# VectorE exponentials as a sum of three shifted 16-bit patterns, in a fused two-branch attention kernel

## The chip, the cores and the metric

The kernel runs on one core of one Trainium2 chip. Its time is device microseconds of one launch; the median of 7 runs of the kernel before is 780.64 us (779.15 to 784.05). Beside it stands one execution recorded by the hardware profiler, and all durations below come from that one.

## The reference, cut to what matters

Two attention branches read the same `x` (2048 rows, 512 columns, 32 heads of 16) and are mixed by a gate. Branch B is softmax attention, branch A is linear attention with a softmax feature map.

```python
def _B_ref(x, wqkv, wo):
    ...
    scores = jnp.einsum("bhqd,bhkd->bhqk", q, k) * (Dh ** -0.5)
    p = _softmax(scores, axis=-1)
    o = jnp.einsum("bhqk,bhkd->bhqd", p, v)
    return (lambda x, *d: x.transpose(*d))(o, 0, 2, 1, 3).reshape(B, S, D) @ wo

g = _sigmoid((x * gate_w).sum(-1, keepdims=True))
a = _A_ref(x, A_wqkv, A_w_phi, A_wo)
b = _B_ref(x, B_wqkv, B_wo)
return g * a + (1 - g) * b
```

What costs most is branch B: 32 heads times 2048 x 2048 scores, each of which needs an exponential. The sum that the softmax divides by is a column of ones beside the values, so numerator and denominator come from the same matmuls, and a common factor on all exponentials cancels.

## The kernel before, in words

**Tiles and blocks.** A tile is 128 keys by 512 queries of one head, so 64 tiles belong to one block of four heads and one query chunk, and there are 32 blocks (`NB`). TensorE makes the scores of a tile with one matmul that uses 32 of the array's rows (`qk_mm`, L782), the exponentials are taken, and TensorE multiplies them with the values, using 32 of its columns per head, into the one accumulator bank `psO` (`pv_mm`, L895). Four matmuls on different 32-row or 32-column strips can run side by side. At the end of a block VectorE copies `psO` out (L979) and the next block starts.

**Two makers of exponentials.** Most tiles go to ScalarE in slots of three and two tiles by turns: `add_qk` fills three PSUM banks (or two), `add_exp` (L874) turns them into bf16 in one of ten parts of `Ebuf`, `add_pv` consumes them some slots later. There are 637 such slots. The other tiles, `DN[b]` of each block and 456 in all, go to VectorE in groups of four (106 groups) or two (16). For one group `add_group` lists: one scores matmul per tile (called dq below) into a spare PSUM bank, D1 (L840) that adds a constant and rounds to int16, so that the 16 bits read as bf16 are a rough power of two; D2 (L855), which takes the low bits and joins a fixed exponent to them; D3 (L857), which keeps the high bits; and D4, which multiplies the first by the second, on VectorE (L860) or, for the first one or two groups of a block (`PN`), on GpSimd in quarters (L863). `add_pvd` then adds two matmuls per tile into `psO`, called terms below: one of the product (`t`) and one of the high bits (`s`).

**Buffers.** Each group holds three buffers of 128 x 2048 bf16: `t`, `s` and the scratch `m`. They come from `rings`, with one set for blocks before `G_EARLY` (13) and one for those after it. `t` and `s` turn through four and four buffers, later four and three. `m` has two fixed ones, one for groups whose product is on VectorE and one for those on GpSimd; it is free again once the product is done. `make_groups` lists a group only when the terms of the earlier holders of its buffers have been listed.

**Order.** All work of all engines is a list of operations with a duration, a priority and dependencies. `layout` runs through them once at build time and fixes the order on every engine; `emit` writes that order out with semaphore waits. [...] When `layout` finds nothing for TensorE and its weighted use over the last 3.41 us is below a bound, it puts in four matmuls of a zero weight (`zero_mm`, L885): they add nothing to the accumulator. VectorE's D2, D3, D4 and GpSimd's tensor operations are marked `lock`, and `layout` doesn't let those of one engine overlap those of the other.

**The rest.** Projections, branch A (its feature map takes 64 more ScalarE exponentials, L1117, sums and products on GpSimd, L1122 and L1130) and the output tiles (`out_tile`, `out_part`, `out_last`; matmuls L590, scaling L1041 and L1065) lie between the slots. The last block ends with a transpose on VectorE, a reciprocal, a product and a second transpose, and then the last matmul of each of the output tiles 12 to 15.

Of the kernel before, what the change touches and what calls it, by code (L numbers as in the profile page):

```python
# [11 lines left out]
ALU = mybir.AluOpType  # L12
# [11 lines left out]
VAW = H * VW + 16  # L24
LOG2E = 1.4426950408889634
QSCALE = 0.25 * LOG2E * 2.0 ** 7
EXPB = 127.0 * 2.0 ** 7 - 75.0
ESCALE = math.log(2.0) / 2.0 ** 7

DN = (0, 10, 14, 16, 14, 16, 14, 16, 14, 16, 14, 16, 14, 16, 14, 16, 14, 16, 14, 16, 14, 16, 14, 16, 14, 16, 14, 16, 14, 16, 14, 12)  # L30
# [72 lines left out]
class Plan:  # L103
# [8 lines left out]
    def add(self, eng, dur, prio, fn, reads=(), writes=(), after=(), name="", sem=None, lat=0.0):  # L112
        op = Op(eng, max(dur - 0.105, 0.05) * DVE_SCALE if eng == "dve" else dur, prio, fn, name)
        if eng == "dve":
            lat += 0.08
        elif eng == "act" and sem is None:
            lat += 0.04
        elif eng == "pe":
            op.dur = max(dur - 0.04, 0.05)
            lat += 0.1  # L120
        op.seq = len(self.ops)
        op.sem, op.lat = sem, lat
        deps = {}
        for k in reads:
            w = self.writer.get(k)
            for x in w or ():
                deps[id(x)] = x
        for k in writes:
            for x in self.writer.get(k) or ():
                deps[id(x)] = x  # L130
            for x in self.readers.get(k, ()):
                deps[id(x)] = x
        for x in after:
            deps[id(x)] = x
        op.deps = list(deps.values())
        for k in reads:
            self.readers.setdefault(k, []).append(op)
        for k in writes:
            self.writer[k] = [op]
            self.readers[k] = []  # L140
        self.ops.append(op)
        return op
# [258 lines left out]
def _build(ctx, nc, A_x, A_wqkv, A_w_phi, A_wo, B_wqkv, B_wo, gate_w, out):  # L401
# [71 lines left out]
    P = Plan()  # L473
# [20 lines left out]
    for rr in range(8):  # L494
# [4 lines left out]
                  name="woa", lat=5.0),  # L499
              dma("sp", 2.2, lambda e: e.dma_start(WoB[:], B_wo.rearrange("(t p) c -> p t c", p=128)), ["WoB"],  # L500
                  name="wob", lat=5.0)]
# [3 lines left out]
    def warm_fn(e):  # L505
        ins = None
        for _ in range(6):
# [5 lines left out]
    pool = lambda dur, prio, fn, reads=(), writes=(), name="": P.add("pool", dur, prio, fn, reads=reads,  # L513
                                                                    writes=writes, name=name)
# [3 lines left out]
         writes=["ident"], name="ident")  # L518
# [9 lines left out]
          writes=["pmask0"], name="pm0")  # L528
    P.add("dve", 0.1, -9, lambda e: e.tensor_scalar(pmask[:, 1:2], pmask[:, 0:1], -QSCALE, QSCALE, op0=ALU.mult,
                                                    op1=ALU.add), reads=["pmask0"], writes=["pmask1"], name="pm1")  # L530
    P.add("dve", 0.1, -9, lambda e: e.tensor_single_scalar(pmask[:, 0:1], pmask[:, 0:1], QSCALE, ALU.mult),
          reads=["pmask1"], writes=["pmask", "pmask0"], name="pm2")
# [6 lines left out]
    for t in range(KT):  # L539
# [12 lines left out]
          writes=["mtmp1"], name="mk0")  # L552
    P.add("dve", 0.12, 30, lambda e: e.tensor_single_scalar(mask64[:], m1, 16, ALU.is_lt), reads=["mtmp1"],
          writes=["mask64"], name="mk1")
    pool(0.3, -2, lambda e: e.tensor_copy(mask4[:], mask64[:].rearrange("p (j c) -> p j c", c=16)[:, :, 0]),
         reads=["mask64"], writes=["mask4"])
# [176 lines left out]
    for j, act in enumerate(slots):  # L733
        for t in act:
            last_act[t[0]] = t
            first_slot.setdefault(t[0], j)
    I16 = mybir.dt.int16
# [6 lines left out]
            "a0": (vfree[:, 0, :], va_free), "a1": (vfree[:, 1, :], va_free),  # L744
            "a2": (vfree[:, 2, :], va_free), "a3": (vfree[:, 3, :], va_free)}
    bufs["pq"], bufs["pt"] = (flat(phiQ[:]), ()), (phiQT[:].rearrange("p g q -> p (g q)"), ())
    rings = ((("x0", "x1", "pq", "o3"), ("y0", "y1", "pt", "o2"), ("woA", "woB")),
             (("x0", "x1", "n0", "a0"), ("y0", "y1", "a1"), ("a2", "a3")))
    for k in range(1):
        bufs[f"n{k}"] = (flat(WAT[:, 4 * k:4 * k + 4, :]), wp_ops)  # L750
# [1 line left out]
    for n, g in enumerate(groups):  # L752
        g["n"], g["ph"] = n, (g["ts"][-1]["t"][0] >= G_EARLY)
        rt, rs, rm = rings[g["ph"]]
        g["m"] = rm[g["pool"]]
        k = count[g["ph"]]
        count[g["ph"]] += 1
        g["t"], g["s"] = rt[k % len(rt)], rs[k % len(rs)]
        for q, d in enumerate(g["ts"]):
            d["g"], d["q"] = g, q  # L760
    opened, phase_ops = set(), [[], []]

    def opening(name):
        if name in opened:
            return []
        opened.add(name)
        return list(bufs[name][1])

    def quarter(ap, q):
        if len(ap.shape) == 3:  # L770
            return ap[:, q // 2, 512 * (q % 2):512 * (q % 2) + 512]
        return ap[:, 512 * q:512 * q + 512]

    def shaped(ap, like):
        return ap.rearrange("p (a c) -> p a c", c=1024) if len(like.shape) == 3 and len(ap.shape) == 2 else ap
# [37 lines left out]
    holder = {}  # L813

    def make_groups(n):
        for g in groups[made[0]:n]:
            if any(k in holder and holder[k]["left"] for k in (g["t"], g["s"])):
                break
            holder[g["t"]] = holder[g["s"]] = g
            add_group(g)  # L820
            made[0] += 1

    def d_prio(d):
        b = d["t"][0]
        return first_slot[b] + d["k"] * 20.0 / DN[b] - D_AHEAD

    def add_group(g):
        t, s, m = (bufs[g[k]][0] for k in "tsm")
        ft, ops, tb = opening(g["t"]), [], t
        before = list(dq_ops)  # L830
        dq_ops.clear()
        for q, d in enumerate(g["ts"]):
            b, i, kt = d["t"]
            f, mm = fill(DQ_PRIO + DQ_K * d_prio(d), [lambda e, ap, t=d["t"]: qk_mm(e, t, ap)],
                         [kkey(b // 8, kt), ("q", b // 2 % 4, b % 2)], name=f"dq{b}.{kt}.{i}", dur=0.25,
                         after=[exp_ops[D_FIRST]] + ft + P.writer.get((g["t"], q), []) +
                         P.readers.get((g["t"], q), []) + before, cols=NQ)
            dq_ops.append(mm)
            mm.kind, mm.heads = "dq", [i]
            ops.append(drain(f, mm, "dve", 0.70, d_prio(d), lambda e, ap, q=q: e.tensor_scalar(  # L840
                quarter(tb, q).bitcast(I16), ap, EXPB, 0.0, op0=ALU.add, op1=ALU.max),
                writes=[(g["t"], q)], after=ft, name=f"D1.{b}.{kt}.{i}"))

        def add(dur, fn, reads, writes, name, after=()):
            ops.append(P.add("dve", dur, d_prio(g["ts"][0]) - 5.0, fn, reads=reads, writes=writes, after=after,
                             name=f"{name}.{b}.{kt}"))
            ops[-1].lock = True
        size = len(g["ts"])
        part = lambda ap: ap[:, 0:512 * size] if len(ap.shape) == 2 else ap[:, 0:size // 2, :]
        t4, m4 = t, m  # L850
        t, s, m = part(t), part(s), part(m)
        tk = [(g["t"], k) for k in range(size)]
        mi, si16, ti16 = m.bitcast(I16), s.bitcast(I16), t.bitcast(I16)
        full = size == 4
        add(0.72 if full else 0.45, lambda e: e.tensor_scalar(shaped(mi, mi), shaped(ti16, mi), 0x007F, 0x3F00, op0=ALU.bitwise_and,  # L855
                                            op1=ALU.bitwise_or), tk, [g["m"]], "D2", opening(g["m"]))
        add(0.72 if full else 0.45, lambda e: e.tensor_single_scalar(shaped(si16, si16), shaped(ti16, si16), 0x7F80, ALU.bitwise_and),  # L857
            tk, [g["s"]], "D3", opening(g["s"]))
        if not g["pool"]:
            add(1.24 if full else 0.72, lambda e: e.tensor_tensor(shaped(t, m), shaped(t, m), m, ALU.mult), [g["m"]], tk, "D4")  # L860
        else:
            for q in range(4):
                ops.append(P.add("pool", 1.1, d_prio(g["ts"][0]) - 5.0, lambda e, q=q: e.tensor_tensor(  # L863
                    quarter(t4, q), quarter(t4, q), quarter(m4, q), ALU.mult), reads=[g["m"]], writes=[tk[q]],
                    name=f"D4{q}.{b}.{kt}"))
                ops[-1].lock = True
        if g is groups[-1]:
            last_d1.extend(ops[:size])
        phase_ops[g["ph"]].extend(ops)
# [28 lines left out]
    def add_pvd(d, started):  # L898
        g, q, (b, i, kt) = d["g"], d["q"], d["t"]
        ops = []  # L900
        for which in "st":
            ap = quarter(bufs[g[which]][0], q)
            op = P.add("pe", 0.25, T_PRIO, lambda e, ap=ap: pv_mm(e, (b, i, kt), ap, False, False),
                       reads=[(g["t"], q) if which == "t" else g["s"], ("v", b // 8, kt // 4), "v1", "v2"],
                       after=[started], name=f"pvd{which}{i}.{b}.{kt}")
            op.full = 0.215
            op.kind, op.heads = "term", [i]
            ops.append(op)
        g["left"] -= 1
        phase_ops[g["ph"]].extend(ops)  # L910
        return ops
# [301 lines left out]
    for i in range(4):  # L1213
        mms = [lambda e, ap, i=i, t=t: e.transpose(ap.bitcast(BF16)[:, 128 * t:128 * (t + 1)],
                                                   xs[:, i, 128 * t:128 * (t + 1)], ident[:]) for t in range(KT)]
        f, mm = fill(-1.0, mms, [("xs", i), "ident"], FIRST, name=f"X{i}", chunk=4, dur=0.08, cols=128)
        x_mms.append(mm)
        dst = xT[:, :, 128 * i:128 * (i + 1)]
# [96 lines left out]
    for op in P.ops:  # L1315
        if op.name.endswith(".0") and op.name[:-2] in gates:
            op.deps = op.deps + [exp_ops[gates[op.name[:-2]]]]
        for head, at, pace in (("P1.", KG_AT, KG_PACE), ("VA", KG_AT, KG_PACE), ("P0.", QG_AT, QG_PACE)):
            part = op.name[len(head):].split(".")
# [38 lines left out]
```

## Time and profile before

| what | value |
|---|---|
| median of 7 runs | 780.64 us (779.15 to 784.05) |
| the profiled execution's own time | 781.83 us |
| span from its first to its last instruction | 780.0 us |
| granted TensorE clock, mean | 0.989 |
| VectorE: D2 (L855), D3 (L857), D4 (L860), busy | 92.0, 88.8, 87.7 us (122, 122 and 75 instructions) |
| GpSimd: D4 in quarters (L863), busy | 215.9 us (188 instructions) |
| TensorE: zero matmuls (L885) | 1764 in the program, 154.2 us busy |
| TensorE: matmuls into `psO` (L895) | 2504 in the program, 239.0 us busy |

The busy time of an engine is the union of its instructions' intervals. Successive instructions of one engine overlap somewhat in this record, so a count times a mean is more than a busy time. The span is 1.8 us shorter than the time of the same execution; the difference lies around the first and the last instruction.

### The profile page before, as it was taken

Reading aid. Unit: us, or ns where it says so; the run is one execution under the profiler, and the core shown is the slowest. Engines: PE = TensorE matmul, PEld = TensorE weight load, DVE = VectorE, ACT = ScalarE, POOL = GpSimd, SP = SyncE. Lnnn points to the kernel's source line nnn. Section 1 sums busy time; section 2 is a strip of 40 time slices with the busy share of each in tenths; the row PEclk is TensorE's granted clock in tenths of the full one; section 3 lists DMA queues with packets and bytes.
Section 4 is the critical chain, followed back from the end, with each engine's and each line's share of the span. In section 5 each row is a group of like instructions: output and inputs, shape, how many; then the busy total and the mean of one; then the engine's idle time right before and its main releaser. Section 6 shows DMA issues by size and latency. Waiting matters only on the chain.

```text
span 780.0 us, 17608 instructions
## 1 busy us (share of the span) xinstructions
PE 741.3 (95%) x7285; PEld 231.3 (30%) x7342; DVE 674.8 (87%) x1098; ACT 758.7 (97%) x708; POOL 352.2 (45%) x329
## 2 busy tenths in 40 slices
PE   8999999999999999999999999999999999999999
PEld 4332223322332222333222232223223223222223
DVE  3678898889989898889999899999999899788793
ACT  6999999999999999999999999999999999989995
POOL 6223634536354564442744636564363544104332
PEclk9999999989999999999999999999999999989999
DMA  7600000000000100201001312331321221020001
GB/s 129 143 9 17 21 13 20 9 18 12 10 17 10 23 8 9 71 9 23 23 23 46 74 56 56 60 68 53 73 66 58 57 63 43 26 52 16 23 21 48
DMA packets 67935, 30.74 MB, mean 39 GB/s; under 512 B 53208, under 2 KB 62808, under 8 KB 67856
## 3 DMA queue, kind: packets, MB, share of 16 engines
q1 hardware_dynamic: 66368, 28.95, 15.7%
q8 instruction: 57, 0.93, 0.5%
q10 hardware_dynamic: 1104, 0.66, 0.3%
q0 software_dynamic: 384, 0.02, 0.1%
q14 instruction: 22, 0.18, 0.1%
HBM read 7.87 MB, written 8.88 MB: 21 GB/s over the span
## 4 chain that ended last, share of the span: by engine, by line
ACT 73%; PE 21%; DVE 4%; issue 1%; DMA 1%; SPq 0%; DVEq 0%
ACT E_t L874 70%; PE psS L782 6%; PE psO L895 5%; ACT EA_t L1117 4%; PE psO L885 3%; PE psS L590 2%; PE psM L590 2%; DVE Tx_t L840 1%; PE psM L782 1%; DMA phiK_t<-in_A_x_dram 1%; DVE vA_t L840 0%; DVE WAT_t L840 0%; DVE oA_t L1205 0%; DVE vA_t L855 0%; DVE Ty_t L857 0%
## 5 line engine op out<-in xcount | busy, mean ns | idle before, releaser
L874 ACT ACTIVATE E_t<-psS 128x1536 bf16<-128x1536 f32 x637 | 729.9, 1339 | 7.8 <-PE psS L782 7.0
L782 PE MATMUL psS<-qz_t,kTB_t 32*128 32x512 bf16 x1816 | 287.3, 387 | 25.6 <-ACT E_t L874 19.2
L863 POOL TENSOR_TENSOR Tx_t<-Tx_t,vA_t 128x512 bf16<-128x512 bf16 x116 | 132.9, 1167 | 124.6 <-DVE Ty_t L857 46.4
L885 PE MATMUL psO<-xT_t,zero_t 128*32 128x512 bf16 x1720 | 151.5, 386 | 0.0
L782 PEld LDWEIGHTS psS<-qz_t,kTB_t 32*128 32x128 bf16 x1816 | 71.4, 91 | 251.7 <-ACT E_t L874 196.1
L895 PE MATMUL psO<-E_t,vaug_t 128*32 128x512 bf16 (+1 forms) x1592 | 140.5, 389 | 0.9 <-issue 0.5
L840 DVE TENSOR_SCALAR Tx_t<-psM 128x512 int16<-128x512 f32 x129 | 87.6, 679 | 12.6 <-PE psM L782 9.7
L840 DVE TENSOR_SCALAR Tx_t<-psS 128x512 int16<-128x512 f32 x119 | 81.2, 682 | 13.4 <-PE psS L782 11.1
L782 PE MATMUL psM<-qz_t,kTB_t 32*128 32x512 bf16 x232 | 89.4, 385 | 1.0 <-DVE qz_t L687 0.5
L863 POOL TENSOR_TENSOR oT_t<-oT_t,WoB_t 128x512 bf16<-128x512 bf16 x44 | 51.2, 1181 | 51.9 <-DVE oT_t L857 28.1
L1122 POOL TENSOR_TENSOR half_t<-EA_t 128x512 f32<-128x512 bf16 x32 | 37.0, 1157 | 63.4 <-ACT EA_t L1117 34.3
L885 PEld LDWEIGHTS psO<-xT_t,zero_t 128*32 128x32 bf16 x1720 | 38.6, 94 | 64.2 <-issue 53.7
L1130 POOL TENSOR_TENSOR phiK_t<-EA_t,stat_t 128x512 bf16<-128x512 bf16 x32 | 34.9, 1090 | 44.3 <-DVE WoB_t L855 13.5
L895 PE MATMUL psO<-Tx_t,vaug_t 128*32 128x512 bf16 x248 | 52.6, 386 | 0.0
L995 POOL TENSOR_TENSOR oT_t<-Tf_t,Rb_t 128x512 bf16<-128x512 f32 x15 | 19.1, 1272 | 70.4 <-DVE vA_t L860 49.8
L895 PEld LDWEIGHTS psO<-E_t,vaug_t 128*32 128x32 bf16 (+1 forms) x1592 | 29.3, 95 | 57.8 <-issue 52.5
L863 POOL TENSOR_TENSOR Tx_t<-Tx_t,WoB_t 128x512 bf16<-128x512 bf16 x28 | 31.8, 1157 | 31.5 <-DVE Ty_t L857 20.7
L1130 POOL TENSOR_TENSOR phiQ_t<-EA_t,stat_t 128x512 bf16<-128x512 bf16 x32 | 33.8, 1057 | 25.3 <-DVE stat_t L1126 8.6
L857 DVE TENSOR_SCALAR Ty_t<-Tx_t 128x2048 int16<-128x2048 int16 x50 | 39.3, 796 | 0.1
L895 PE MATMUL psO<-Ty_t,vaug_t 128*32 128x512 bf16 (+1 forms) x284 | 38.7, 386 | 0.0
L782 PEld LDWEIGHTS psM<-qz_t,kTB_t 32*128 32x128 bf16 x232 | 21.1, 91 | 34.1 <-issue 13.1
L840 DVE TENSOR_SCALAR WAT_t<-psM 128x512 int16<-128x512 f32 x39 | 26.6, 683 | 4.2 <-PE psM L782 3.8
(184 smaller groups left out, 888.6 us busy)
## 6 DMA issues: line engine op xcount, KB each, us to landing
dpq<-phiQ_t SPq DMA_DIRECT2D x16, 256.0 KB, 2.2
Rb_t<-lr SPq DMA_DIRECT2D x120, 32.0 KB, 1.8
dpo<-oA_t SPq DMA_DIRECT2D x16, 128.0 KB, 1.9
qz_t<-qz_t SPq DMA_DIRECT2D x120, 16.0 KB, 1.8
Tf_t<-Tf_t SPq DMA_DIRECT2D x60, 32.0 KB, 2.0
out_dram<-WvA_t SPq DMA_DIRECT2D x14, 128.0 KB, 1.7
WB_t<-in_B_wqkv_dram SPq DMA_DIRECT2D x3, 384.0 KB, 4.4
WvA_t<-in_A_wqkv_dram SPq DMA_DIRECT2D x1, 512.0 KB, 4.1
```

The source lines that it names most:

```text
L590: return [lambda e, ap, i=i: e.matmul(ap, lhsT=lhs[i], rhs=rhs[i], start=(i == 0), stop=(i == len(lhs) - 1)) for i in range(len(lhs))]
L782: return e.matmul(bank, lhsT=kT_B[32 * i:32 * i + 32, b // 8 % 2, 128 * kt:128 * (kt + 1)], rhs=qz[32 * i:32 * i + 32, b // 2 % 4, b % 2, ...
L840: ops.append(drain(f, mm, "dve", 0.70, d_prio(d), lambda e, ap, q=q: e.tensor_scalar(quarter(tb, q).bitcast(I16), ap, EXPB, 0.0, op0=ALU.a ...
L857: add(0.72 if full else 0.45, lambda e: e.tensor_single_scalar(shaped(si16, si16), shaped(ti16, si16), 0x7F80, ALU.bitwise_and), tk, [g["s ...
L863: ops.append(P.add("pool", 1.1, d_prio(g["ts"][0]) - 5.0, lambda e, q=q: e.tensor_tensor(quarter(t4, q), quarter(t4, q), quarter(m4, q), A ...
L874: op = P.add("act", 0.051 + 0.4267 * n, 0.0, lambda e: e.activation(Ebuf[:, j // 2 % EPAIRS, 1536 * (j % 2):1536 * (j % 2) + 512 * n], psS ...
L885: ins = e.matmul((psO if bank is None else bank)[32 * i:32 * i + 32, :], lhsT=zero[:], rhs=xT[:, 0, 0:NQ], start=bank is not None, stop=ba ...
L895: return e.matmul(psO[32 * i:32 * i + w, :], lhsT=vaug[:, kt, o:o + w], rhs=rhs, start=start, stop=stop, tile_position=(0, 32 * i), skip_g ...
L995: P.add("pool", 1.1, -40, lambda e: e.tensor_tensor(oT[:, r, qc, :], Tf[:, 0, :], Rb[:], ALU.mult), reads=[("Tf", 0), "Rb"], writes=[("oT" ...
L1117: ins = e.activation(EA[:, b, :].rearrange("p (g s c) -> p s g c", s=2, c=64)[:, sgn, :, :], ap.rearrange("p (g c) -> p g c", c=64), ACTF. ...
L1122: P.add("pool", 1.15, prio, lambda e: e.tensor_tensor(half[:], e3[:, :, 0:8], e3[:, :, 8:16], ALU.add), reads=[("EA", b)], writes=["half"] ...
L1130: parts.append(P.add("pool", 1.0, prio, lambda e, n=n: e.tensor_tensor(dst[:, 512 * n:512 * n + 512].rearrange("p (g f) -> p g f", f=DH), ...
```

## The change

The exponential of a VectorE tile is made in another way. D1 stays, with another constant. Instead of splitting the 16 bits and multiplying, the pattern is taken three times: as it is (`t`), with 35 added to the integer (`s`), and with 83 added (`m`). Each of the three read as bf16 is a rough, scaled power of two whose error runs differently within an octave, and the sum of the three is what goes into the softmax. The sum is made by TensorE: three terms per tile in place of two. The product on VectorE or GpSimd is gone.

`m` is now read by TensorE too, so it is held as long as `t` and `s`. It gets a ring of its own: three buffers before block 13 (`woA`, `woB`, and `o2`, which the `s` ring gives up) and two from there on (`a2`, `a3`). `s` then turns through three buffers in both. `PN`, which said which products go to GpSimd, no longer decides anything; `DN`, the number of VectorE tiles per block, is the same.

```diff
-EXPB = 127.0 * 2.0 ** 7 - 75.0
+EXPB = 127.0 * 2.0 ** 7 - 252.7
+STEPS = (35, 83)
...
-    rings = ((("x0", "x1", "pq", "o3"), ("y0", "y1", "pt", "o2"), ("woA", "woB")),
+    rings = ((("x0", "x1", "pq", "o3"), ("y0", "y1", "pt"), ("woA", "woB", "o2")),
              (("x0", "x1", "n0", "a0"), ("y0", "y1", "a1"), ("a2", "a3")))
...
-        g["m"] = rm[g["pool"]]
...
-        g["t"], g["s"] = rt[k % len(rt)], rs[k % len(rs)]
+        g["t"], g["s"], g["m"] = rt[k % len(rt)], rs[k % len(rs)], rm[k % len(rm)]
...
-            if any(k in holder and holder[k]["left"] for k in (g["t"], g["s"])):
+            if any(k in holder and holder[k]["left"] for k in (g["t"], g["s"], g["m"])):
                 break
-            holder[g["t"]] = holder[g["s"]] = g
+            holder[g["t"]] = holder[g["s"]] = holder[g["m"]] = g
...
-        add(0.72 if full else 0.45, lambda e: e.tensor_scalar(shaped(mi, mi), shaped(ti16, mi), 0x007F, 0x3F00, op0=ALU.bitwise_and,
-                                            op1=ALU.bitwise_or), tk, [g["m"]], "D2", opening(g["m"]))
-        add(0.72 if full else 0.45, lambda e: e.tensor_single_scalar(shaped(si16, si16), shaped(ti16, si16), 0x7F80, ALU.bitwise_and),
-            tk, [g["s"]], "D3", opening(g["s"]))
-        if not g["pool"]:
-            add(1.24 if full else 0.72, lambda e: e.tensor_tensor(shaped(t, m), shaped(t, m), m, ALU.mult), [g["m"]], tk, "D4")
-        else:
-            for q in range(4):
-                ops.append(P.add("pool", 1.1, d_prio(g["ts"][0]) - 5.0, lambda e, q=q: e.tensor_tensor(
-                    quarter(t4, q), quarter(t4, q), quarter(m4, q), ALU.mult), reads=[g["m"]], writes=[tk[q]],
-                    name=f"D4{q}.{b}.{kt}"))
-                ops[-1].lock = True
+        for key, dst, step in (("s", s, STEPS[0]), ("m", m, STEPS[1])):
+            add(0.72 if size == 4 else 0.45, lambda e, dst=dst, step=step: e.tensor_single_scalar(dst, t, step, ALU.add),
+                tk, [g[key]], "D2" if key == "s" else "D3", opening(g[key]))
...
-        for which in "st":
+        for which in "tsm":
             ap = quarter(bufs[g[which]][0], q)
             op = P.add("pe", 0.25, T_PRIO, lambda e, ap=ap: pv_mm(e, (b, i, kt), ap, False, False),
-                       reads=[(g["t"], q) if which == "t" else g["s"], ("v", b // 8, kt // 4), "v1", "v2"],
+                       reads=[(g["t"], q) if which == "t" else g[which], ("v", b // 8, kt // 4), "v1", "v2"],
```

Since the order on every engine is laid out anew from the changed list, instructions move on all of them, the untouched ones too.

More of the change, by code (lines that the diff above doesn't have):

```diff
@@ L848, in add_group @@
         size = len(g["ts"])
-        part = lambda ap: ap[:, 0:512 * size] if len(ap.shape) == 2 else ap[:, 0:size // 2, :]
-        t4, m4 = t, m
+        part = lambda ap: ap[:, 0:512 * size].bitcast(I16)
         t, s, m = part(t), part(s), part(m)
         tk = [(g["t"], k) for k in range(size)]
-        mi, si16, ti16 = m.bitcast(I16), s.bitcast(I16), t.bitcast(I16)
-        full = size == 4
-        add(0.72 if full else 0.45, lambda e: e.tensor_scalar(shaped(mi, mi), shaped(ti16, mi), 0x007F, 0x3F00, op0=ALU.bitwise_and,
-                                            op1=ALU.bitwise_or), tk, [g["m"]], "D2", opening(g["m"]))
-        add(0.72 if full else 0.45, lambda e: e.tensor_single_scalar(shaped(si16, si16), shaped(ti16, si16), 0x7F80, ALU.bitwise_and),
-            tk, [g["s"]], "D3", opening(g["s"]))
-        if not g["pool"]:
-            add(1.24 if full else 0.72, lambda e: e.tensor_tensor(shaped(t, m), shaped(t, m), m, ALU.mult), [g["m"]], tk, "D4")
-        else:
-            for q in range(4):
-                ops.append(P.add("pool", 1.1, d_prio(g["ts"][0]) - 5.0, lambda e, q=q: e.tensor_tensor(
-                    quarter(t4, q), quarter(t4, q), quarter(m4, q), ALU.mult), reads=[g["m"]], writes=[tk[q]],
-                    name=f"D4{q}.{b}.{kt}"))
-                ops[-1].lock = True
+        for key, dst, step in (("s", s, STEPS[0]), ("m", m, STEPS[1])):
+            add(0.72 if size == 4 else 0.45, lambda e, dst=dst, step=step: e.tensor_single_scalar(dst, t, step, ALU.add),
+                tk, [g[key]], "D2" if key == "s" else "D3", opening(g[key]))
         if g is groups[-1]:
```

## The prediction

> **What bounds the kernel now.** I read first the busy times and the slices of the page, then the groups.
>
> ```profile
> PE 741.3 (95%) x7285; PEld 231.3 (30%) x7342; DVE 674.8 (87%) x1098; ACT 758.7 (97%) x708; POOL 352.2 (45%) x329
> ...
> ACT  6999999999999999999999999999999999989995
> ...
> PEclk9999999989999999999999999999999999989999
> ...
> ACT 73%; PE 21%; DVE 4%; issue 1%; DMA 1%; SPq 0%; DVEq 0%
> ...
> L874 ACT ACTIVATE E_t<-psS 128x1536 bf16<-128x1536 f32 x637 | 729.9, 1339 | 7.8 <-PE psS L782 7.0
> ```
>
> ScalarE (ACT) is busy in 97% of the span, and its 637 exponentials have only 7.8 us of idle time before them. TensorE's 95% is not its need: 154.2 us of it are zero matmuls that `layout` put in where nothing was ready. The pace of ScalarE is in the chain of waits:
>
> ```profile
> 512.23 29.38 ACT E_t L874 x26
> 541.61 0.98 ACT EA_t L1117 x2
> ```
>
> 26 exponentials in 29.38 us are 1.130 each without a gap; a pair of feature-map exponentials takes 0.98. So 637 x 1.130 + 32 x 0.98 = 751 us must pass on ScalarE. The first exponential starts at 10.2, the last ends at 770.9, and the tail is 9.1. 10.2 + 751 + 9.1 = 770.5; the other 9.5 us of the span are stalls: 1.7 at the first exponential, some 1.3 scattered, and about 6.5 in two places. The timeline of ScalarE and the windows show them:
>
> ```profile
> 682.96 1.02 ACT L874 ACTIVATE E_t<-psS 128x1024 bf16<-128x1024 f32 x1 [0.17 <-PE psS L782]
> 685.13 2.53 ACT L874 ACTIVATE E_t<-psS 128x1536 bf16<-128x1536 f32 x2 [1.14 <-PE psS L782]
> 688.92 20.50 ACT L874 ACTIVATE E_t<-psS 128x1536 bf16<-128x1536 f32 x18 [1.26 <-PE psS L782]
> ```
>
> ```profile
> core 0: us, PE busy (x) PEld busy (x) DVE busy (x) ACT busy (x) POOL busy (x), PEclk, DMA share, GB/s
> 155.28:162.11 6.83, 6.10 (x62) 2.34 (x54) 6.83 (x11) 6.83 (x8) 5.50 (x5) 1.00 0.01 4
> 162.11:168.94 6.83, 6.36 (x39) 1.18 (x39) 4.18 (x8) 5.73 (x6) 2.26 (x3) 0.50 0.10 20
> 680.94:687.77 6.83, 6.83 (x45) 1.27 (x42) 3.20 (x6) 5.35 (x5) 3.44 (x4) 0.50 0.33 78
> 708.24:711.65 3.41, 3.41 (x15) 0.59 (x17) 2.26 (x4) 2.63 (x3) 1.15 (x1) 0.50 0.02 2
> ```
>
> In three stretches the granted TensorE clock is 0.50. There, and almost only there, ScalarE waits for scores: the idle times are 5.3 us (eight gaps, the third stretch's among them), and as exponentials overlap by 0.1 to 0.2 at their seams, each gap costs that much more than it shows, some 1.2 in all. So the kernel is bound by ScalarE, plus some 2.2 us per half-clock stretch.
>
> **What is removed.** On VectorE (DVE) D2, D3 and D4, 92.0 + 88.8 + 87.7 = 268.5 us busy; on GpSimd (POOL) 188 products, 215.9 us. None is waited for by ScalarE: with VectorE idle for 105 us and GpSimd for 428, they lie under the exponentials. By itself this removes 0 us of the span.
>
> **What is added on VectorE.** 244 integer adds, 212 of 2048 elements and 32 of 1024. No such add is in the trace. The nearest row is D3, one source and one destination of the same size and 16-bit type, and one operation with a constant:
>
> ```profile
> L857 DVE TENSOR_SCALAR vA_t<-Tx_t x12: 680/683/1164, 356.0 to 723.5; 128x2048 int16<-128x2048 int16 x12
> L857 DVE TENSOR_SCALAR phiQT_t<-phiQ_t x12: 413/418/687, 42.4 to 311.9; 128x1024 int16<-128x1024 int16 x7, 128x2048 int16<-128x2048 int16 x5
> ```
>
> The columns are shortest, median and longest ns: 0.68 us undisturbed, up to 1.16 beside GpSimd. At 0.68 and 0.42 the adds take 212 x 0.68 + 32 x 0.42 = 158 us; at D3's mean (88.8 / 122 = 0.73) 178. I take 158, since GpSimd's load falls from 352 to 136 us. VectorE then falls to 675 - 268 + 158 = 565 us. [...] Nothing on the path either way.
>
> **What is added on TensorE.** 456 more terms. Rows of zero matmuls in the timeline give the price: 8 take 0.61 us and 4 take 0.39, so a further set of four on four column strips costs 0.22. In the built order the 1368 terms stand in 371 sets, the 912 of before in 244: 127 x 0.22 = 28 us. Score matmuls for VectorE tiles ride more often beside others (153 sets of their own, before 220): -67 x 0.22 = -15. Zero sets fall from 441 to 364: -17. So the need rises by 13 us and filler pays for it. [...] Summing need between successive score matmuls of the built order, by 0.22 per set and 0.1 for a change of strips (a scores matmul to the next `psO` matmul is 0.32 in the timeline), eight slots (9.04 us of ScalarE) are overrun at five starting points, at worst by 0.47; before it is three, by 0.46. I charge 0.4 us; ends 0 and 1.5.
>
> **What waits.** D3 of a group now waits for the terms of the group two (later blocks) or three before. Behind it on VectorE stand D1s, the `psO` copy and the K and Q drains; if these were late, the next block's accumulation would be. In the built order the values matmuls of a slot stand at most 7 score sets behind (before 9) of a ring of 10 `Ebuf` parts, so the order has room: 0, upper end in rival E.
>
> **The tail.** In the order before, all eight matmuls of output tile 11 stand between the second last and the last `psO` set:
>
> ```profile
> 770.56 0.81 PE L590 MATMUL psM<-WoA_t,phiK_t 128*128 128x512 bf16 x3 [0.16 <-issue]
> 771.21 1.03 PE L590 MATMUL psM<-WoB_t,oT_t 128*128 128x512 bf16 x4
> 772.16 0.39 PE L895 MATMUL psO<-E_t,vaug_t 128*32 128x512 bf16 x2
> ```
>
> The last exponential ends at 770.9, its `psO` set starts at 772.16. In the new order tile 11 is done before, seven matmuls of tile 12 (7 x 0.22 = 1.5 us) stand there instead from about 770.0, and the last sets follow at 771.5. After them come 7 matmuls, not 14, so the closing matmul of tile 12, today 0.4 us behind its input (775.14 to 775.52), isn't held up either. I take 0.9; ends 0 and 1.2.
>
> **The sum.** Against the profiled execution's 781.83: -0.9 + 0.4 = -0.5, so 781.3 with as many half-clock stretches. The median, 780.64, is 1.2 below that execution; with the same -0.5 I predict **780.1 us**, no change that can be told (the bound is 0.3%, 2.3 us).
>
> [...] Over three successive slots (about one 3.4 us step, by which the stretches are spaced), the new order has about the same mean work as the old, and slightly more in its thinnest twentieth; but its thinnest places are wider: around exponentials 284, 322 and 480 two or three neighbouring windows are thin. I expect three stretches again, plus or minus two.
>
> **Rivals.**
> - B, the clock drops more often: the wide thin places are hit in most runs. Price 2.2 each; two more make 780.1 + 4.4 = 784.5, slower. It decides from the second on. For it: the widths; against: more terms fill other windows. 0.22.
> - C, it drops less often: two fewer make 775.7, faster. The spread of the seven runs, 4.9 us, is about two stretches. 0.20.
> [...]
> - E, two `m` buffers are too few: D3 heads VectorE's queue while 12 terms (three sets, 0.7 us, with slots between) drain. If each of the 19 later blocks lost 0.5 us, 789.6. Against it: VectorE gains 110 us of room. 0.07.
>
> **Chances.** The forecast 0.48: 0.44 within the bound, 0.04 faster. Faster 0.20 + 0.04 = 0.24, same 0.44, slower 0.22 + 0.07 + 0.03 = 0.32. The forecast's own range is 778 to 782.5. For eight in ten I reach to C's and B's cases: 774.5 to 787.
>
> **What would show it.** Right: 637 exponentials at 1.130 with idle time only in half-clock stretches; VectorE near 565 us, GpSimd near 136, adds of 0.68; zero matmuls down by about 300; the last `psO` set within 0.8 us of the last exponential. Wrong: adds over 1 us undisturbed, ScalarE waiting for scores at full clock, or many more or fewer stretches at 0.50.

## The result and the profile after

The changed kernel takes **778.49 us** (median of 11 runs, 774.81 to 779.59). The kernel before, run beside it and in a larger number this time, takes 782.41 (26 runs, 777.88 to 786.13). The ratio is **0.9942, 95% interval 0.9922 to 0.9961**: 0.6% faster, about 4.5 us. The forecast was 780.1 and "no change that can be told"; the time lies in its range, but the kernel got faster by more than the 0.3% that it named. The forecast change was -0.5 us and the measured one about nine times that. That 780.1 came so near to 778.49 is in part luck: the seven runs that it started from had a median of 780.64, 1.8 us below that of the later runs.

The lines of the page of the changed kernel that answer to those shown before (L862 is now the exponential on ScalarE, L853 an integer add, L873 a zero matmul, L883 a matmul into `psO`):

```profile
PE 733.2 (95%) x7431; PEld 229.5 (30%) x7490; DVE 585.3 (75%) x1023; ACT 757.3 (98%) x708; POOL 137.2 (18%) x141
...
PEclk9999999999999999999999999999999999999999
...
L862 ACT ACTIVATE E_t<-psS 128x1536 bf16<-128x1536 f32 x637 | 731.3, 1383 | 4.6 <-PE psS L782 4.1
```

VectorE lost 90 us and GpSimd 215, and ScalarE's busy time is what it was. Its idle time before exponentials fell from 7.8 to 4.6 us, 1.7 of that at the first one in both. The PEclk row has no 8 left. The windows of the changed kernel, at its three half-clock stretches:

```profile
398.24:401.65 3.41, 3.41 (x23) 0.61 (x27) 2.90 (x6) 3.08 (x4) 0.00 (x0) 0.50 0.20 43
589.39:592.80 3.41, 3.41 (x25) 0.97 (x27) 0.68 (x2) 2.81 (x3) 0.00 (x0) 0.50 0.18 40
681.55:684.96 3.41, 3.41 (x35) 0.61 (x31) 1.39 (x2) 2.40 (x3) 0.00 (x0) 0.50 0.27 70
```

The columns are those of the windows before: the stretch, its length, busy time and count of PE, PEld, DVE, ACT and POOL, then the granted clock. There are three stretches as in the kernel before, but each is one step of 3.41 us; before, two of them were two steps long. So TensorE ran at half clock for 10.2 us in place of 17.1.

The span fell from 780.0 to 775.7. It can be cut at the first and the last exponential:

| part, one profiled execution each | before | after | difference |
|---|---|---|---|
| start to first exponential | 10.2 | 11.5 | +1.3 |
| exponentials at their own pace, and their first waits | 751.3 | 751.2 | -0.1 |
| stalls of ScalarE in and just behind half-clock stretches | 6.7 | 3.3 | -3.4 |
| other stalls of ScalarE | 2.7 | 1.5 | -1.1 |
| last exponential's end to the end | 9.1 | 8.1 | -1.0 |
| span | 780.0 | 775.7 | -4.3 |

A stall is how much more time than the median of its form passed from the end of the activation before to the end of this one. The start isn't the change's doing: the profiles of the twelve variants below have 9.9 to 12.1 there, in those of the kernel before as in those of the changed one.

Each run also comes with a mean granted clock, so the half-clock steps of every run can be counted: (1 - clock) x span / 1.71 us, rounded. Over the 56 comparison runs of the kernel before the mean is 4.8 steps (3 to 8), and a straight line through their times is 776.7 + 1.23 us per step, with a standard error of 0.11 on the price. Over 12 runs of the changed kernel, the profiled one included, it is 3.3 steps (2 to 4). The line there, 774.6 + 0.98 per step, has standard errors of 1.7 and 0.5 and tells little. The difference of the means is 782.6 - 777.9 = 4.7 us. At 1.23 a step, 1.8 of it is the 1.4 steps fewer, and 1.0 is the tail as the two profiles have it. The other 1.9 us, cheaper steps or stalls elsewhere, these runs don't divide.

### The profile page after: what moved, and what is told of

The parts are those of the page before. It is cut to its first block, busy times and chain, and to the rows that moved or that the text cites. A ratio compares the mean times of both kernels' runs of the same rounds, so it can differ in the third digit from the quotient of the medians.

```text
span 775.7 us, 17650 instructions
## 1 busy us (share of the span) xinstructions
PE 733.2 (95%) x7431; PEld 229.5 (30%) x7490; DVE 585.3 (75%) x1023; ACT 757.3 (98%) x708; POOL 137.2 (18%) x141
## 3 DMA queue, kind: packets, MB, share of 16 engines
q1 hardware_dynamic: 66368, 28.95, 15.8%
## 4 chain that ended last, share of the span: by engine, by line
ACT 84%; PE 13%; DVE 2%; issue 1%; DMA 1%; SPq 0%
ACT E_t L862 81%; PE psS L782 4%; ACT EA_t L1105 4%; PE psO L883 4%; PE psM L591 1%; PE psO L873 1%; PE psS L591 1%; PE psM L651 1%; DMA phiK_t<-in_A_x_dram 1%; DVE Tx_t L840 0%; DVE WAT_t L840 0%; PE psM L782 0%; PE psS L1219 0%; PE psM L873 0%; DVE Tf_t L967 0%
## 5 line engine op out<-in xcount | busy, mean ns | idle before, releaser
L862 ACT ACTIVATE E_t<-psS 128x1536 bf16<-128x1536 f32 x637 | 731.3, 1383 | 4.6 <-PE psS L782 4.1
L782 PE MATMUL psS<-qz_t,kTB_t 32*128 32x512 bf16 x1815 | 276.5, 386 | 28.6 <-ACT E_t L862 22.0
L782 PEld LDWEIGHTS psS<-qz_t,kTB_t 32*128 32x128 bf16 x1815 | 68.7, 91 | 262.8 <-ACT E_t L862 227.6
L883 PE MATMUL psO<-E_t,vaug_t 128*32 128x512 bf16 (+1 forms) x1592 | 140.7, 387 | 0.5 <-issue 0.3
L873 PE MATMUL psO<-xT_t,zero_t 128*32 128x512 bf16 x1372 | 119.6, 386 | 0.0
L883 PE MATMUL psO<-vA_t,vaug_t 128*32 128x512 bf16 (+1 forms) x430 | 58.9, 388 | 0.0
L883 PE MATMUL psO<-Ty_t,vaug_t 128*32 128x512 bf16 (+1 forms) x308 | 50.2, 387 | 0.0
L883 PEld LDWEIGHTS psO<-E_t,vaug_t 128*32 128x32 bf16 (+1 forms) x1592 | 28.9, 95 | 59.3 <-issue 56.5
L873 PEld LDWEIGHTS psO<-xT_t,zero_t 128*32 128x32 bf16 x1372 | 31.1, 94 | 51.4 <-issue 42.3
L883 PE MATMUL psO<-Tx_t,vaug_t 128*32 128x512 bf16 (+1 forms) x248 | 38.0, 396 | 0.0
L853 DVE TENSOR_SCALAR vA_t<-Tx_t 128x2048 int16<-128x2048 int16 x50 | 34.3, 690 | 0.1
L853 DVE TENSOR_SCALAR Ty_t<-Tx_t 128x2048 int16<-128x2048 int16 x42 | 29.8, 710 | 0.4
L840 DVE TENSOR_SCALAR WAT_t<-psS 128x512 int16<-128x512 f32 x39 | 26.6, 682 | 2.3 <-PE psS L782 2.0
```

The costliest lines, as they stand in the source:

```text
L782: return e.matmul(bank, lhsT=kT_B[32 * i:32 * i + 32, b // 8 % 2, 128 * kt:128 * (kt + 1)], rhs=qz[32 * i:32 * i + 32, b // 2 % 4, b % 2, ...
L853: add(0.72 if size == 4 else 0.45, lambda e, dst=dst, step=step: e.tensor_single_scalar(dst, t, step, ALU.add), tk, [g[key]], "D2" if key ...
L862: op = P.add("act", 0.051 + 0.4267 * n, 0.0, lambda e: e.activation(Ebuf[:, j // 2 % EPAIRS, 1536 * (j % 2):1536 * (j % 2) + 512 * n], psS ...
L873: ins = e.matmul((psO if bank is None else bank)[32 * i:32 * i + 32, :], lhsT=zero[:], rhs=xT[:, 0, 0:NQ], start=bank is not None, stop=ba ...
L883: return e.matmul(psO[32 * i:32 * i + w, :], lhsT=vaug[:, kt, o:o + w], rhs=rhs, start=start, stop=stop, tile_position=(0, 32 * i), skip_g ...
```

## The experiments

Three theories stood against each other for what lies beyond the tail. *Terms*: the 456 further matmuls keep TensorE fuller, so its clock drops less. *Relief*: VectorE and GpSimd have less to do. *Layout*: the drops follow thin places of the order that `layout` writes, whatever made them. Thin places are counted in the built order, not in the profile: the weighted use that `layout` itself gives to sets of matmuls, summed over three successive slots (about 3.4 us). Of those windows, the kernel before has 18 below 2.0 and 28 below 2.2, the changed one 15 and 19; the mean is 3.3 in both.

**Three terms on the old VectorE work.**

```diff
 # kernel before
-        for which in "st":
+        for which in "sts":
```

> The kernel before, with the term of the high bits multiplied in twice (three terms per tile as in the change; the sums are weighted otherwise than the reference's). VectorE and GpSimd keep their old work, TensorE gets the change's 456 further matmuls. Theory of the terms (the gain is from TensorE being fuller, so that its clock drops less): half-clock time falls from 17 to about 10 us, ratio 0.994 to 0.997 although its tail is worse (13 output matmuls stand between the last scores and the last values). Theory of the relief (the gain is from VectorE and GpSimd being emptier, so that nothing waits for them): no gain, ratio 1.000 to 1.006. Theory of the layout (half-clock stretches follow the thin places of the order laid out, whatever made them; here 12 windows of three slots under 1.8 of weighted use, before 7, changed kernel 8): as many stretches as before or more, ratio 1.002 to 1.006 with the tail 1 to 1.5 us longer.

Ratio 1.0039 (1.0021 to 1.0057), 785.31 us; 4.6 half-clock steps on the mean, 17.1 us in the profiled run. The terms alone win nothing. The zeros explain why: `layout` put in 339 sets where it had 433, so the terms took the place of filler.

**Two terms on the new VectorE work.**

```diff
 # changed kernel
-        for which in "tsm":
+        for which in "ts":
```

> The changed kernel without the third term (the pattern plus 83 is made but not multiplied in, so the exponentials of VectorE are a sum of two). TensorE has the term count of before, VectorE and GpSimd are as in the change. Theory of the terms: stretches come back to 17 us, only the tail's 1 us stays: ratio 0.998 to 1.000. Theory of the relief: the whole gain stays, 0.993 to 0.995, with idle time of ScalarE at full clock as low as in the change. Theory of the layout (3 thin windows under 1.8, 4 under 2.0): half-clock time 0 to 7 us, ratio 0.990 to 0.994.

Ratio 0.9900 (0.9878 to 0.9922), 774.99 us, 1.8 steps. Faster than the change itself by 0.4%, so the terms of the change win nothing. Whether they cost anything by themselves is not shown: the new order of a_two has 490 sets of zeros where the change has 357, and a_fill11 below, with all three terms and as few steps (1.8), is at 0.9912. The theory of the terms is out; relief and layout stand.

**The tail alone.**

```diff
 # kernel before
-OP_AT = 620.0
+OP_AT = 400.0
```

> The kernel before with the due time of the two partial output tiles moved from 620 to 400, which only takes output matmuls out of its last slots: in the new order seven matmuls of tile 12 are spread before the last values sets and 7 follow, as in the change. Theory of the tail: last exponential to end falls from 9.1 to about 8.2 us, ratio about 0.9985; the rest stays (5 thin windows under 1.8, 16 under 2.0, as before), half-clock time 14 to 20 us. Should the tail not shrink, the 0.9 us of the prediction was not the order of the output matmuls.

Ratio 0.9975 (0.9954 to 0.9996), 781.17 us, 4.5 steps; from the last exponential to the end 7.7 us in place of 9.1. The tail is worth what the order of its output matmuls says, and no more than about a fifth to a third of the gain.

**Without the product.** This one takes out what the change takes out and adds nothing.

```diff
 # kernel before
-        if not g["pool"]:
-            add(1.24 if full else 0.72, lambda e: e.tensor_tensor(shaped(t, m), shaped(t, m), m, ALU.mult), [g["m"]], tk, "D4")
-        else:
...
```

> The kernel before with the product left out (VectorE's 75 and GpSimd's 188 multiplications are not done, so the term of the product is the raw pattern; the two bit passes and the two terms per tile stay). If what the change removes is what it gains by, and the third term gives nothing: ratio 0.992 to 0.996, the number of 3.4 us half-clock windows falls from a mean of 4.8 to 2 to 4, and ScalarE's other stalls fall by about 1 us. If the third term is needed for the gain: 0.998 to 1.001 with 4 to 5 windows.

Ratio 0.9967 (0.9948 to 0.9986), 780.51 us, 4.3 steps. The kernel is faster, although its profile has 11.2 us from the last exponential to the end, 2.1 more than before. That isn't the order of the output matmuls, for the first closing one starts 4.6 us behind the last exponential in both. One of the last transfers of the output landed 4.0 us after its issue; in the kernel before none took more than 2.3. The lines for the output transfers, first of the kernel before (L1024), then of this one (L1016):

```profile
DMA to landing us min/median/max: 1.7/1.7/2.3
DMA to landing us min/median/max: 1.7/1.7/4.0
```

Whether the other runs of this kernel have so late a transfer isn't known. ScalarE's stalls are 5.8 us in place of 9.4 (after the change 4.9), in one profile each:

```profile
L866 ACT ACTIVATE E_t<-psS 128x1536 bf16<-128x1536 f32 x637 | 730.9, 1378 | 5.5 <-PE psS L782 3.3
```

So in these profiles taking the product away gives most of the change's gain between the first and the last exponential. The number of steps goes only from 4.8 to 4.3 (standard errors 0.2 and 0.3), less than expected and not clear of noise; one of the five in its profile stands behind the last exponential, where none waits. The thin places of the order don't foretell that. One count for all three built orders, from each scores set to the third next, comes out somewhat higher than the one above: 22 and 37 windows below 2.0 and 2.2 in the kernel before, 17 and 25 in the changed one, 13 and 20 here. This kernel has the fewest thin places of the three, but more steps than the changed one.

**More and fewer zeros in the changed kernel.** Four kernels change how `layout` fills, and nothing of the work.

```diff
 # changed kernel; a_fill, a_fill11, a_act07, a_ahead18
-ACTIVE = (1.0, 0.64, 0.62, 0.54)
+ACTIVE = (1.6, 0.64, 0.62, 0.54)
+ACTIVE = (1.1, 0.64, 0.62, 0.54)
+ACTIVE = (0.7, 0.64, 0.62, 0.54)
+ACTIVE = (1.2, 0.64, 0.62, 0.54)
 # a_ahead18 only
-D_AHEAD = 22.0
+D_AHEAD = 18.0
```

> The changed kernel with the bound under which the layout puts in zero matmuls raised from 1.0 to 1.6: 429 sets of zeros in place of 357, 4 thin windows under 1.8 in place of 8, 8 under 2.0 in place of 15. Theory of the layout: half-clock time falls to 0 to 7 us and the ratio to 0.989 to 0.993. Theories of the terms and of the relief: VectorE, GpSimd and the terms are those of the change, so 0.994 as the change, give or take the tail (tile 11 ends one matmul later: under 0.5 us).

> The changed kernel with the bound for zero matmuls raised from 1.0 to 1.1 alone: 420 zero sets, 3, 6 and 8 windows under 1.8, 2.0 and 2.2 in place of 8, 15 and 19; the order of its tail is the change's, so 8.1 us. Theory of the layout: 1 to 2.5 half-clock windows on the mean in place of 3.3, ratio 0.988 to 0.992. If thin windows of the order don't set the count: 3 to 4 windows, 0.992 to 0.996.

> The changed kernel with the bound for zero matmuls lowered from 1.0 to 0.7: 187 zero sets in place of 357, 19 windows of three slots under 2.0 of weighted use in place of 15, 48 under 2.2 in place of 19. VectorE, GpSimd and the terms do what they do in the change. If thin TensorE work is what drops the clock and a drop is what costs the time: 5 to 8 half-clock windows on the mean, about 1.0 to 1.4 us each, ratio 0.997 to 1.003. If relief of VectorE and GpSimd by itself shortens ScalarE's waits: 0.993 to 0.996 whatever the zeros.

> The changed kernel with the bound for zeros at 1.2 and VectorE tiles due 18 slots ahead in place of 22: 432 zero sets, 1, 3 and 11 windows under 1.8, 2.0 and 2.2. Its tail is the longer one (six matmuls of tile 11 before the last values sets and 14 of tiles 12 and 13 behind), 9 to 10 us. Theory of the layout: 0.5 to 2 half-clock windows, so the base of the change with 1 us more of tail: 0.989 to 0.993. If thin windows don't set the count: 3 to 4 windows, 0.994 to 0.998.

| kernel | windows below 2.0 / 2.2 | half-clock steps, mean | ratio (95% interval) |
|---|---|---|---|
| before | 18 / 28 | 4.8 | 1 |
| changed | 15 / 19 | 3.3 | 0.9942 (0.9922 to 0.9961) |
| a_fill, bound 1.6 | 8 / 12 | 2.5 | 0.9914 (0.9889 to 0.9939) |
| a_fill11, bound 1.1 | 6 / 8 | 1.8 | 0.9912 (0.9887 to 0.9936) |
| a_ahead18, bound 1.2, 18 slots ahead | 3 / 11 | 0.7 | 0.9912 (0.9898 to 0.9927) |
| a_act07, bound 0.7 | 19 / 48 | 4.1 | 0.9956 (0.9928 to 0.9983) |

Among these kernels the steps go where the thin windows go: same VectorE work, same terms, 3.3 to 0.7 steps. The page of a_ahead18 and its timeline show ScalarE without a clock to wait for:

```profile
L862 ACT ACTIVATE E_t<-psS 128x1536 bf16<-128x1536 f32 x637 | 729.6, 1370 | 2.0 <-PE psS L782 1.7
```

```profile
659.81 103.05 ACT L862 ACTIVATE E_t<-psS 128x1536 bf16<-128x1536 f32 x91
```

All but 0.3 us of its idle time is the wait at the first exponential, and the last 91 exponentials run in one piece. It is no faster than a_fill11. Its profile has a tail of 10.0 us where that has 8.1, most of it again one late output transfer (3.6 us at the longest, 2.3 in a_fill11).

The other direction missed: with the bound at 0.7 I expected 5 to 8 steps and a ratio of at least 0.997, and got 4.1 (1 to 7 over its runs) and 0.9956. That ratio lies where the theory of relief had put it, 0.993 to 0.996. A count of windows below 2.2 says too little when most of the new ones lie just below it. But within its 12 runs the time follows the steps, 772.8 + 1.43 us per step with a standard error of 0.14. This price, with the new VectorE work, is no lower than the 1.23 of the kernel before.

**No zeros at all**, in both kernels, so that the layout can't make up for terms that aren't there.

```diff
 # both kernels
-ACTIVE = (1.0, 0.64, 0.62, 0.54)
+ACTIVE = (0.0, 0.0, 0.0, 0.54)
```

> The changed kernel without any zero matmul in the layout. 182 windows of three slots have a weighted use under 2.2 (with zeros 19). If thin TensorE work drops the clock and a drop costs ScalarE 1.0 to 1.4 us per 3.4 us: 15 to 50 half-clock windows and a ratio of 1.01 to 1.06. If the further terms alone keep TensorE full enough for the clock: no more than 6 windows, 0.994 to 1.000. If the clock isn't what costs the time: windows as may be, ratio 0.993 to 0.997, since zeros add nothing to the result.

> The kernel before without any zero matmul in the layout; 237 windows under 2.2 (with zeros 28). Compared with the changed kernel without zeros it tells what the 456 further terms do for the clock when the layout doesn't make up for them. If they fill TensorE: 20 to 60 half-clock windows, at least a quarter more than in the changed kernel without zeros, and a ratio of 1.02 to 1.08, at least 0.01 above it. If they don't matter: window counts within a tenth of each other, and the two ratios apart by the 0.003 to 0.006 that they are with zeros.

Changed kernel: ratio 1.0792 (1.0773 to 1.0811), 843.83 us. Kernel before: 1.0873 (1.0848 to 1.0897), 851.03 us. Both are slower than I had thought, with 82 and 83 half-clock steps. First two lines of the kernel before without zeros, then one of the changed kernel without them:

```profile
PEclk9888788998969798899878797768797667887979
...
L874 ACT ACTIVATE E_t<-psS 128x1536 bf16<-128x1536 f32 x637 | 736.9, 1293 | 61.1 <-PE psS L782 49.4
```

```profile
L862 ACT ACTIVATE E_t<-psS 128x1536 bf16<-128x1536 f32 x637 | 735.7, 1300 | 49.9 <-PE psS L782 44.0
```

The zeros add nothing to any sum and are worth 65 us in the changed kernel and 69 in that of before. The terms don't replace them: the step counts agree within a fiftieth. The two ratios are 0.008 apart, about what they are with zeros (0.006) or a little more. With as many steps in both, these 7 us can't come from fewer steps; something else of the change is worth time here.

**More tiles for VectorE**, since the change frees it.

```diff
 # both kernels, 28 blocks from the third on
-14, 16, 14, 16, ...
+16, 18, 16, 18, ...
```

> The changed kernel with 16 and 18 VectorE tiles in the blocks that have 14 and 16: 56 tiles go from ScalarE to VectorE, 615 slots in place of 637, 168 more terms. If ScalarE stays the bound: 22 slots by 1.130 are 24.9 us less, ratio 0.962 to 0.968. If TensorE's order becomes the bound (in the order laid out the values matmuls stand up to 10 score sets behind, and 28 output matmuls have moved behind the last slot): 0.975 to 0.995, with the tail 6 us longer and ScalarE waiting for scores.

> The kernel before with the same 16 and 18 VectorE tiles per block. VectorE is 87% busy and has to take 56 tiles of about 1.3 us more, 748 us of a span that would have to be 755: if VectorE's work is what kept tiles on ScalarE, ratio 0.985 to 1.01, worse than the changed kernel at the same tiles by 0.01 or more. If VectorE isn't the limit there: equal to the changed kernel at these tiles within 0.004.

Changed kernel: 1.0336 (1.0309 to 1.0363), 809.02 us; kernel before: 1.0866 (1.0839 to 1.0893), 850.55 us. Both lose, against what I expected of either. ScalarE of the changed kernel is busy 21.5 us less than at the change's own tiles, but its exponentials wait 46 us, most of it for something that they didn't wait for there (us in total, times, longest):

```profile
ACT E_t L862 <- PE psO L883: 39.8, 12, 15.8
```

That is an exponential that can't be written because its part of `Ebuf` still waits for its values matmul: 12 times, at longest 15.8 us. The kernel before waits in the same place at these tiles, 73.3 us in 26 times, so the new ring of `m` can't be the whole reason. In the longest wait, from 352.0 to 367.9, TensorE has single scores matmuls for VectorE's tiles, terms and zeros. For all but the first 1.9 us of it VectorE works nearly without a break, 13.78 of 13.94 us (the third busy time):

```profile
353.93:367.87 13.94, 13.94 (x165) 4.58 (x157) 13.78 (x25) 0.01 (x1) 0.00 (x0) 1.00 0.00 1
```

So there the end of the block waits for VectorE's pace. The other eleven waits were not followed up. At these tiles the change is worth 41 us, at its own tiles 4.5.

## Why the prediction was right or wrong

**The bound: right.** ScalarE's pace per exponential is unchanged (751.3 and 751.2 us for all of them and their first waits), and the whole change of the span lies outside it.

**VectorE and GpSimd: sizes about right.** The row of the adds in the changed kernel:

```profile
L853 DVE TENSOR_SCALAR vA_t<-Tx_t x50: 628/682/1169, 339.1 to 740.6; 128x2048 int16<-128x2048 int16 x50
```

0.68 us as D3 has, 160.5 us for the 244 where 158 was charged. The chances add 0.03 to 0.22 and 0.07 for a slower kernel; no run shows this term, and what the runs showed in its place is adds at D3's 0.68 us. VectorE's 585 is 20 above the 565, of which 15 are instructions that stand less tightly and so overlap less in the record (55.5 us in all, before 70.6). GpSimd's 137 was forecast as 136.

**The further terms: right that they cost little.** Zero matmuls fell by 77 sets, and a_two, which lacks the third term, gains no more than 0.4% on the changed kernel (0.9900 to 0.9942, the intervals just touch). In the trace of the kernel before one zero matmul takes 386 ns on the mean, a set of four on four column strips 0.39 us, of eight 0.61 and of sixteen 1.05, so four more take 0.22 us more together. Four scores matmuls, which use 32 rows each, take 0.39 in the second of these lines:

```profile
170.44 1.05 PE L885 MATMUL psO<-xT_t,zero_t 128*32 128x512 bf16 x16
...
171.63 0.39 PE L782 MATMUL psS<-qz_t,kTB_t 32*128 32x512 bf16 x4
...
689.66 0.61 PE L885 MATMUL psO<-xT_t,zero_t 128*32 128x512 bf16 x8
...
691.31 0.39 PE L885 MATMUL psO<-xT_t,zero_t 128*32 128x512 bf16 x4
```

**What waits: right at 0.** The adds on VectorE did wait for terms, longer than D3 had in the kernel before (0.5 us). The line has VectorE's idle time before them in us, and the number of waits:

```profile
  PE psO L883: 11.0, 8
```

ScalarE's stalls away from the drops fell all the same, from 2.7 to 1.5 us, so rival E, with its 9.5 us, is out.

**The tail: right.** -0.9 forecast, -1.0 measured in the two profiles. The lines of the changed kernel's TensorE timeline:

```profile
766.82 1.04 PE L591 MATMUL psM<-WoA_t,phiK_t 128*128 128x512 bf16 x4
767.69 0.81 PE L591 MATMUL psM<-WoB_t,oT_t 128*128 128x512 bf16 x3
768.43 0.40 PE L883 MATMUL psO<-E_t,vaug_t 128*32 128x512 bf16 x4
...
771.17 0.39 PE L591 MATMUL psM<-WoB_t,oT_t 128*128 128x512 bf16 x1 [0.73 <-DVE oT_t L1002]
```

The last exponential ends at 767.5; the last values set starts 0.9 us later (before: 1.3; the sign named was 0.8). The closing matmul of tile 12 now waits for its input, where before the input waited for it.

**What is removed: wrong at 0 us.** "By itself this removes 0 us of the span" looked at who waits for the product, and ScalarE never does. But b_nomul, which removes only the product, gains 0.3% (0.1 to 0.5). The prediction read the new order for the terms, the tail and the thin places, but its sum has no term for what an emptier VectorE does to ScalarE's stalls. How that gain comes about is not shown in full. In the profiles a half-clock microsecond costs ScalarE 0.39 us in the kernel before, 0.31 in b_nomul and 0.33 in the changed one; the prices over many runs don't bear that out (1.23 us per step in the kernel before, 1.43 in a_act07).

**The clock: the step that failed.** "I expect three stretches again" was true of the profile and of no use, for a stretch isn't a unit: 17.1 us before and 10.2 after. The steps of 3.41 us are, and over all runs they went from 4.8 to 3.3. The orders showed it beforehand, with 28 thin windows and 19; the prediction weighed three places more where thin windows lie side by side. Two of the three, near exponentials 322 and 480, are indeed where the profile's drops begin (326 and 483), but the number of drops is not set by them alone. The price per stretch, 2.2 us, hid the same mistake: it is 1.2 per step. So rival C, fewer drops, took place in part. That its price of 4.4 us for two stretches fewer is close to the measured gain is luck: the 1.4 steps fewer are 1.8 us of it, and 1.0 is the tail.

**Half clock without long gaps.** In the kernel before without zeros TensorE never idles for more than 1.35 us after the first 20 us, and its clock is at half for a third of the time (mean 0.836). These are the steps just before the three drops of the kernel before:

```profile
158.70:162.11 3.41, 2.84 (x23) 0.84 (x19) 3.41 (x7) 3.41 (x4) 3.41 (x4) 1.00 0.01 2
677.53:680.94 3.41, 2.46 (x30) 0.88 (x31) 3.41 (x10) 3.41 (x4) 1.05 (x1) 1.00 0.12 41
704.83:708.24 3.41, 2.35 (x12) 0.82 (x14) 3.41 (x7) 3.41 (x4) 0.00 (x0) 1.00 0.01 2
```

TensorE is busy in 83, 72 and 69% of them, with no gap over 0.63 us. The 6.10 of 6.83 us in the windows of the kernel before, from 155.28 to 162.11, took in a fuller step before, 3.27 of 3.42. In the kernel before without zeros it is 73% at the median of 37 drops (48 to 88%), and 93% in the steps that left the clock full (67 to 100%). As these ranges overlap, a bound can't be read off. Whether it is the plain busy time or the weighted use that counts, the runs don't tell.

What stays open: why the order with less work on VectorE meets fewer drops, since b_nomul has few thin places and hardly fewer steps; where the 1.9 us go that are neither steps nor tail; and whether a half-clock step is cheaper where VectorE is emptier, on which single profiles and prices over many runs disagree.

The fastest version run that keeps the change's sum of three, a_fill11, is the change with one constant: 774.67 us, ratio 0.9912, against 0.9942 of the change. The intervals of the two overlap.

## What to carry to other kernels

Where ScalarE is full, ask of a change elsewhere what it does to the few microseconds in which ScalarE waits, and count these in the unit that they come in, over all runs and not in one profile. Work taken off an engine that nobody waits for can still move the time where a planner lays everything out anew (0.3% in b_nomul). Before freed time is used for more work, look at the stretches and not at the mean: VectorE was busy 75% of the span, and the tiles given to it came back as waits of ScalarE, in the longest of them behind a VectorE that was busy 13.78 of 13.94 us.

## What the runs showed of the hardware that was not expected

The clock of TensorE went to half without any long gap: in the kernel before without zero matmuls TensorE was busy 89% of the span with no gap over 1.35 us after the first 20 us, and the step before a drop was busy 73% at the median. Without the zero matmuls the mean clock was 0.836 and 0.845 in the profiles, and it cost 65 and 69 us of about 780; with enough of them in the right places (a_ahead18) it was 1.000. In the nine profiles with drops of kernels with zeros and the old number of VectorE tiles, 19 of 23 drops stand within eight exponentials behind a place that is among the thinnest 2.5% of its kernel's windows in the built order. The other four are in kernels whose bound for zeros was changed.
